# A list-scheduled attention and feed-forward kernel: other planner costs, 600 random trials of its priorities, and masks made by GpSimd and ScalarE

## The chip, the cores and the metric

One core of a Trainium2 chip runs the whole program. The metric is the device time of one execution in microseconds. The kernel before takes 627.38 us, the median of three runs (626.61 to 627.97).

## The reference

Sliding-window attention with sink keys is followed by a two-matrix feed-forward layer with an ELU between the matrices.

```python
batch, n_heads, seq, head_dim = (4, 8, 768, 64);  n_sink, window = (4, 128)
scores = scale * np.matmul(q, k.transpose(0, 1, 3, 2))
keep = is_sink | in_window                 # key < n_sink, or 0 <= query - key < window
a = softmax(np.where(keep, scores, -1e9))
x = np.matmul(a, v)                        # transposed and reshaped to 3072 tokens x 512
h = x @ w_in                               # 512 x 2048
g = np.where(h > 0.0, h, np.exp(np.minimum(h, 0.0)) - 1.0)
return g @ w_out                           # 2048 x 512
```

## The kernel before, in words

**Chunks.** The 24 query tiles of 128 tokens are cut into nine chunks of 2, 2, 2 and then 3 tiles (`SIZES`). For each chunk the attention of all heads makes `x`, and then the feed-forward layer runs over 16 slices of the hidden dimension: per slice, 12 matmuls into `h` (stage 1, L765) and, two slices later, the matmuls into `acc` (stage 2, L793). The first two chunks are taken in parts (`PARTS`): slices 0 to 6 of chunk 0, 0 to 12 of chunk 1, then the rest of both. A slice needs two pieces of weights.

**Attention of chunk 0.** Four pairs of heads with two query tiles each make eight units. A unit is: scores on PE (L601, `s`), a masked minimum on DVE (L616, `e`), exponentials on ACT (L618), a small addition on POOL or ACT (L622), a reciprocal on DVE (L623), a diagonal matrix on POOL (L630, `pq`), a product with it on PE that turns the probabilities round (L636, `acc`), a copy (L640, `pt`), and the product with the values on PE (L653, `po`). There are two score banks. There are two key buffers (`kqs`); those of pairs 2 and 3 are loaded into the buffers of pairs 0 and 1 once their scores are done (L516). Later chunks split the probabilities into two halves of float16 (L668, L669), turn them round by a DMA transpose (L687), and take the sinks' part on POOL (L675 to L679).

**Weights.** Each of the 32 pieces is loaded (L314, `raw`), split by ACT (L307, `wu`), DVE (L308, `wv`) and ACT (L456), and its low half is made by two subtractions on POOL (L457, `w`).

**Masks and parameters.** `n_sink` and `window` arrive by DMA, are cast by DVE (L1110), spread over the partitions by a small matmul (L1111) and copied back (L1112). `make_masks` makes the distances on POOL and DVE (L331 to L337) and the masks from them on DVE (L345, L348). PE takes the small matmul before the first scores.

**What sets the order.** Nothing above is issued in the order in which it is written. Every piece of work is a `Task` with an engine, a duration (`act_us`, `dve_us`, `pool_us` or a number), dependencies, and for PE a position. `Plan.order` gives each task a due time, counted back from the PE position of what needs it, and runs a list scheduler: an engine that is free takes, of what is ready, what is due first. This is repeated 8 times, each time with the PE times of the last round, and the round with the earliest end is kept. `HOP` is the planner's delay from one engine to the next. `keep_order` then pins the order of each engine to that plan, so that the engines wait for each other by semaphores but never swap instructions. Where the plan has PE idle in its first 100 us, `with_idle_products` puts products of a constant matrix on PE (L882, `hot`), as many as fill 60% of the gap at `IDLE_US` each.

**End.** A check of the ranges of all inputs runs beside the work. A second, general path is not taken here.

Of the kernel before, what the change touches and what calls it, by code (L numbers as in the profile page):

```python
# [12 lines left out]
I32 = mybir.dt.int32  # L13
# [7 lines left out]
P = 128  # L21
# [7 lines left out]
NS = 4  # L29
# [18 lines left out]
ROUNDS = 8  # L48
VISIT = 3
# [3 lines left out]
IDLE_US, IDLE_FILL, IDLE_UNTIL, IDLE_LEAST = 0.11, 0.6, 100.0, 0.8  # L53
# [3 lines left out]
PE_T, PE_V = 0.25, 0.25  # L57
# [46 lines left out]
class Plan:  # L104


    HOP = {"PE": 0.15, "ACT": 0.08, "DVE": 0.08, "POOL": 0.2, "SP": 0.0}
# [30 lines left out]
    def order(self):  # L138
# [7 lines left out]
        for _ in range(ROUNDS):  # L146
            self.backward()
            end = self.forward(pe)
            if VERBOSE:
                print("round", end)  # L150
            if best is None or end < best[0]:
                best = end, [(t.start, t, t.eng) for t in self.tasks]
        self.end = best[0]
        for s, t, e in best[1]:
            t.take(e)
            t.start = s
        return [t for _, t, _ in sorted(best[1], key=lambda v: (v[0], v[1].n))]
# [126 lines left out]
def act_us(n, scaled=False):  # L284
    return 0.17 + 0.00088 * n + (0.08 if scaled else 0.0)


def dve_us(n):
    return 0.12 + 0.00115 * n


def pool_us(n):
    return 0.18 + 0.0019 * n
# [32 lines left out]
def make_masks(nc, tmp, sk, low, m0, m1, m2):  # L326


    ri = tmp[:, 0:P].bitcast(I32)
    rel, own, prev = (tmp[:, i * P : (i + 1) * P] for i in (1, 2, 3))  # L330
    nc.gpsimd.iota(ri, pattern=[[-1, P]], base=0, channel_multiplier=1)  # L331
    for j in range(NS):
        nc.gpsimd.memset(sk[:, j : j + 1], float(j))
# [32 lines left out]
def fast_path(tc, ctx, first, kq, vx, wt, out, low, spread, numbers, flag):  # L366
# [36 lines left out]
    spread(po_ps[0])  # L403
# [4 lines left out]
    tmp = pts[-1].rearrange("p b k -> p (b k)").bitcast(F32)  # L408
    second, rest = make_masks(nc, tmp[:, : 4 * P], tmp[:, 4 * P : 4 * P + NS], low, m0, m1, m2)
    nc.gpsimd.memset(ones, 1.0)  # L410
    for t in wu:
        nc.gpsimd.memset(t, 0)
    nc.gpsimd.memset(hot, 1.0)
    make_identity(nc, ident)
# [11 lines left out]
    second_ = add("DVE", 0.65, second)  # L426
    rest_ = add("DVE", 0.5, rest)
    numbers_ = add("DVE", 1.3, numbers)
# [12 lines left out]
    def weights(k):  # L441
# [3 lines left out]
        ld = add("SP", 0.4, lambda: load_weights(nc, raw, wt[k]), deps=[w_done.get(k - AHEAD, [None])[0]], lat=1.45)  # L445
        if wide:
            steps = weight_f32(nc, v, top, raw, 2.0)
            a = add("ACT", act_us(512), steps[0], deps=[ld])
            b = add("DVE", 0.13 + 0.00108 * 512, steps[1], deps=[a], slow=1.5)
# [45 lines left out]
    def attention(c):  # L495
# [12 lines left out]
        def split_keys(h):  # L508
# [4 lines left out]
            if c < DUP:  # L513
                ld = None
                if (c, h) not in first["kq"]:
                    ld = add("SP", 0.4, lambda: nc.sync.dma_start(st[:, :kw], kq[:, o : o + kw]), lat=dma_us(P * kw * 4) * 1.15)  # L516
                users = []
                return st, None, ld, ld, users
# [653 lines left out]
```

## Time and profile before

| | |
|---|---|
| median of three runs | 627.38 us |
| the profiled execution, its own time | 628.19 us |
| its span, first to last instruction | 626.3 us |
| PE busy | 606.1 us (97%) |
| DVE, ACT, POOL busy | 462.3, 421.2, 294.7 us |

The share of busy time is a mean over stages that have different limits, so the rows below are by stage. The stages are cut at 4.98 us, where the first scores run on PE, and at 32.69 us, where the first matmul of the feed-forward layer runs.

### The profile page before, as it was taken

What the parts mean: (1) busy time and instruction counts of PE and PEld (TensorE: products, weight loads), DVE (VectorE), ACT (ScalarE), POOL (GpSimd) and SP (SyncE); (2) the same over time, 40 slices, a digit from 0 to 9 for tenths busy, and PEclk for the clock granted to TensorE, in tenths of its full rate; (3) what the DMA queues carried; (4) which work ended last, traced back from release to release, by engine and by line L of the source; (5) the groups of instructions that cost most, each with busy time, mean ns of one, the idle gap of its engine ahead of it and who ended that gap; (6) DMA issues with size and microseconds to landing.
All of it is one profiled execution on the core that took longest, in us unless ns stands there. A gap on an engine that the chain in (4) does not pass through costs nothing.

```text
span 626.3 us, 13397 instructions
## 1 busy us (share of the span) xinstructions
PE 606.1 (97%) x4504; PEld 359.4 (57%) x4504; DVE 462.3 (74%) x1206; ACT 421.2 (67%) x1192; POOL 294.7 (47%) x595
## 2 busy tenths in 40 slices
PE   6997999999999999999999999999999999999995
PEld 4664665667675555555555555555555555555552
DVE  7877677979878786688788988788877887543323
ACT  5887888879878876676667666676767666432221
POOL 4876689875445444344344445334324444222221
PEclk9898999999999999999999999999999999999998
DMA  8698977758656665586456865676655864413101
GB/s 293 210 248 199 298 243 192 209 139 223 145 127 157 162 146 103 94 216 181 125 153 177 230 139 159 130 197 136 166 125 124 209 144 107 115 50 92 55 2 53
DMA packets 122077, 98.24 MB, mean 157 GB/s; under 512 B 98324, under 2 KB 98324, under 8 KB 122004
## 3 DMA queue, kind: packets, MB, share of 16 engines
q1 hardware_dynamic: 122004, 97.34, 60.7%
q8 instruction: 37, 0.61, 0.4%
q14 instruction: 36, 0.29, 0.2%
HBM read 66.38 MB, written 7.34 MB: 118 GB/s over the span
## 4 chain that ended last, share of the span: by engine, by line
PE 91%; POOL 3%; DVE 2%; issue 2%; DMA 1%; ACT 1%; POOLq 0%; ACTq 0%
PE acc L793 39%; PE h L765 38%; PE po L701 5%; PE s L595 2%; PE s L596 2%; PE s L601 2%; POOL w L457 1%; PE h L882 1%; PE acc L636 1%; DMA pt<-pq 1%; DMA vs<-in_vx_dram 1%; PE po L706 1%; PE po L653 0%; DVE pt L334 0%; POOL pq L630 0%
## 5 line engine op out<-in xcount | busy, mean ns | idle before, releaser
L765 PE MATMUL h<-x,w 128*128 128x384 f16 (+1 forms) x1728 | 274.9, 309 | 2.4 <-DVE g L776 2.3
L765 PEld LDWEIGHTS <-w 128*128 128x128 f16 x1728 | 168.3, 98 | 94.8 <-issue 3.2
L786 POOL TENSOR_TENSOR gl<-g,gh 128x384 f16<-128x384 f32 (+1 forms) x144 | 128.7, 894 | 157.3 <-ACT gh L779 134.2
L793 PE MATMUL acc<-w,gh 128*128 128x512 f16 x768 | 192.7, 379 | 1.0 <-POOL w L457 1.0
L773 ACT ACTIVATE g<-h 128x384 f32<-128x384 f32 (+1 forms) x144 | 65.1, 452 | 101.8 <-PE h L765 92.2
L793 PEld LDWEIGHTS <-gh 128*128 128x128 f16 x768 | 72.9, 98 | 69.4 <-issue 0.9
L793 PE MATMUL acc<-w,gl 128*128 128x512 f16 x384 | 109.2, 379 | 0.0
L669 DVE SCALAR_TENSOR_TENSOR pq<-e,st,pq 128x256 f16<-128x256 f32 (+1 forms) x176 | 95.1, 571 | 13.0 <-ACT pq L668 12.7
L618 ACT ACTIVATE e<-e,st 128x264 f32<-128x264 f32 (+1 forms) x192 | 92.9, 484 | 12.2 <-DVE st L616 11.2
L779 ACT ACTIVATE gh<-g 128x384 f16<-128x384 f32 (+1 forms) x144 | 69.3, 481 | 43.2 <-DVE g L776 41.5
L616 DVE CUSTOM_DVE_ANT_0 e<-s,m 128x264 f32<-128x264 f32 (+1 forms) x192 | 71.7, 405 | 26.2 <-PE s L596 19.8
L776 DVE SCALAR_TENSOR_TENSOR g<-g,h 128x384 f32<-128x384 f32 (+1 forms) x144 | 72.8, 506 | 13.2 <-POOL g L775 11.3
L668 ACT ACTIVATE pq<-e,st 128x256 f16<-128x256 f32 (+1 forms) x176 | 77.1, 482 | 5.3 <-DVE st L623 4.1
L775 POOL TENSOR_SCALAR g<-g 128x384 f32<-128x384 f32 (+1 forms) x80 | 41.5, 518 | 80.2 <-ACT g L773 79.8
L775 DVE TENSOR_SCALAR g<-g 128x384 f32<-128x384 f32 (+1 forms) x64 | 26.8, 419 | 65.7 <-ACT g L773 65.4
L793 PEld LDWEIGHTS <-gl 128*128 128x128 f16 x384 | 37.5, 98 | 46.6 <-POOL gl L786 0.9
L524 ACT ACTIVATE kq<-kqs 128x780 f16<-128x780 f32 (+1 forms) x48 | 42.7, 901 | 15.7 <-PE s L596 12.2
L457 POOL TENSOR_TENSOR w<-wv,w 128x256 f16<-128x256 f32 x64 | 49.2, 789 | 5.4 <-ACT w L456 4.7
L622 POOL TENSOR_SCALAR st<-st 128x2 f32<-128x2 f32 x84 | 21.2, 253 | 48.0 <-ACT e L618 44.1
L701 PE MATMUL po<-pt,vh 128*64 128x128 f16 x656 | 35.8, 221 | 2.6 <-DVE x L740 1.9
L618 ACT ACTIVATION_READ_ACCUMULATOR e<-e,st 128x1 f32 x192 | 36.1, 188 | 0.0
L595 PE MATMUL s<-kq 128*128 128x264 f16 (+1 forms) x144 | 34.3, 267 | 0.6 <-ACT x L739 0.6
(92 smaller groups left out, 628.8 us busy)
## 6 DMA issues: line engine op xcount, KB each, us to landing
raw<-in_wt_dram SPq DMA_DIRECT2D x32, 512.0 KB, 4.8
kqs<-in_kq_dram SPq DMA_DIRECT2D x24, 456.0 KB, 3.6
kqs<-in_kq_dram SPq DMA_DIRECT2D x24, 390.0 KB, 3.6
vs<-in_vx_dram SPq DMA_DIRECT2D x28, 256.0 KB, 3.6
out_dram<-wv SPq DMA_DIRECT2D x24, 256.0 KB, 2.6
vm<-in_kq_dram SPq DMA_DIRECT2D x24, 228.0 KB, 3.7
vm<-in_kq_dram SPq DMA_DIRECT2D x24, 195.0 KB, 3.4
vm<-in_vx_dram SPq DMA_DIRECT2D x6, 768.0 KB, 5.3
```

The costliest lines, as they stand in the source:

```text
L616: red = add("DVE", 0.24 + 0.001 * wd, lambda ee=ee, me=me, sp=sps[e], m=m, wd=wd, to_score=to_score: nc.vector.tensor_tensor_reduce(ee, sp ...
L618: ex = add("ACT", 0.47 + 0.00085 * wd, lambda ee=ee, me=me, rs=rs[:, e : e + 1]: nc.scalar.activation(ee, ee, AF.Exp, bias=me, scale=-1.0, ...
L668: a = add("ACT", act_us(nb * P, True), lambda src=src, hi=hi, re=re: nc.scalar.activation(hi, src, AF.Copy, scale=re), deps=[rr])
L669: b = add("DVE", 0.478 if nb == 2 else 0.33, lambda src=src, hi=hi, lo=lo, re=re: nc.vector.scalar_tensor_tensor(lo, src, re, hi, ALU.mult ...
L701: nc.tensor.matmul(po[e * D : (e + 1) * D, oc], vts[i][x][:, vo : vo + D], pt[:, (2 * e + part) * nb + i, :], start=new, stop=last)
L765: nc.tensor.matmul(hp[:, :n], win[:, part, d, :], xx[:, :n], start=k == 0, stop=k == 3 * ND - 1)
L773: a = add("ACT", act_us(n) + 0.18, lambda gf=gf, hp=hp, sums=sums: nc.scalar.activation(gf, hp[:, :n], AF.Exp, scale=1.0 / G_SCALE, accum_ ...
L775: b = add("DVE", 0.14 + 0.00057 * n, lambda gf=gf: nc.vector.tensor_scalar(gf, gf, -1.0, G_SCALE, ALU.add, ALU.mult), deps=[a], slow=2.1, ...
L776: b = add("DVE", dve_us(n), lambda gf=gf, hp=hp: nc.vector.scalar_tensor_tensor(gf, gf, 0.0, hp[:, :n], ALU.min, ALU.max), deps=[b])
L779: th = add("ACT", act_us(n), lambda gf=gf, gh=gh: nc.scalar.activation(gh[:, :n], gf, AF.Copy), deps=[b])
L786: tls.append(add("POOL", pool_us(cut), lambda gl=gl, gf=gf, gh=gh, cut=cut: nc.gpsimd.tensor_tensor(gl[:, :cut], gf[:, :cut], gh[:, :cut], ...
L793: nc.tensor.matmul(acc[i], gg[:, i * P : (i + 1) * P], wout[:, part, :], start=f == f0 and k == 0, stop=f == f1 - 1 and k == 2)
```

## The change

It alters five things; the line numbers below are of the kernel before.

1. All durations in the plan, and the delays `HOP`. Most become smaller; the DMA transposes become longer.
2. After the eight rounds come 600 further ones (`SEARCH`). Each takes the best plan so far, shifts by random amounts the due times of the tasks in some stretch of it (or all), or the PE positions of one kind of work, schedules again, and keeps the result if its planned end is no later.
3. The masks: GpSimd makes both distances itself, in float32. DVE keeps the comparisons. ScalarE casts the two parameters. In the plan the masks for units 1 and 2 follow the minimum of units 0 and 1, and the check of the parameters (`numbers`) follows the first exponentials of the feed-forward layer.
4. The first keys are the first DMA; the parameters follow them.
5. The constant products before 12 us of the plan are planned at twice the time, so fewer fit. For chunks 3 to 8 the small addition of L622 is always on POOL. The small matmul of the parameters stands first on PE by a pinned order.

```diff
-PE_T, PE_V = 0.25, 0.25
+PE_T, PE_V = 0.25, 0.13
...
-    HOP = {"PE": 0.15, "ACT": 0.08, "DVE": 0.08, "POOL": 0.2, "SP": 0.0}
+    HOP = {"PE": 0.2, "ACT": 0.14, "DVE": 0.125, "POOL": 0.09, "SP": 0.0}
...
+        draw = random.Random(1)
+        for _ in range(SEARCH):
+            _, due, ideal, then = best
+            for t, d, s in zip(self.tasks, due, then):
+                t.due, t.start = d, s[0]
+            for t, i in zip(pe, ideal):
+                t.ideal = i
+            a, w, by = draw.uniform(0.0, 200.0), draw.choice((5.0, 15.0, 40.0)), draw.choice((0.5, 2.0, 6.0))
+            kind = draw.random()
+            if kind < 0.65:
...
+                for t, s in zip(self.tasks, then):
+                    if a <= s[0] < a + w:
+                        t.due += draw.gauss(0.0, by)
+            else:
...
+            best = self.better(best, pe)
...
 def act_us(n, scaled=False):
-    return 0.17 + 0.00088 * n + (0.08 if scaled else 0.0)
+    return 0.085 + 0.000855 * n + (0.095 if scaled else 0.0)
...
 def dve_us(n):
-    return 0.12 + 0.00115 * n
+    return 0.067 + 0.00105 * n
...
-    ri = tmp[:, 0:P].bitcast(I32)
-    rel, own, prev = (tmp[:, i * P : (i + 1) * P] for i in (1, 2, 3))
-    nc.gpsimd.iota(ri, pattern=[[-1, P]], base=0, channel_multiplier=1)
...
-    nc.vector.tensor_copy(rel, ri)
-    nc.vector.tensor_scalar(own, rel, 0.0, 1.0e6, ALU.is_lt, ALU.mult)
-    nc.vector.tensor_tensor(own, own, rel, ALU.add)
-    nc.vector.tensor_scalar(prev, rel, float(P), None, ALU.add)
+    own, prev = tmp[:, 0:P], tmp[:, P : 2 * P]
+    nc.gpsimd.iota(own, pattern=[[-1, P]], base=0, channel_multiplier=1, **exact)
+    nc.gpsimd.affine_select(out=own, in_=own, compare_op=ALU.is_ge, fill=1.0e6, base=0, pattern=[[-1, P]], channel_multiplier=1)
...
+    nc.gpsimd.iota(prev, pattern=[[-1, P]], base=P, channel_multiplier=1, **exact)
...
+                if c < DUP:
+                    rr = add("ACT", 0.18, eps[0], deps=[ex for _, ex in exps], or_=("POOL", 0.21, eps[1]))
+                else:
+                    rr = add("POOL", 0.21, eps[1], deps=[ex for _, ex in exps])
...
+            us = IDLE_US if t.start > COLD_UNTIL else 2 * IDLE_US
...
-            nc.vector.tensor_copy(t[0:1, :], ints[0:1, :])
+            nc.scalar.activation(t[0:1, :], ints[0:1, :], AF.Copy)
...
+            if n == "kqs" and i == 0:
+                nc.sync.dma_start(ints[0:1, 0:2], n_sink.bitcast(I32))
+                nc.sync.dma_start(ints[0:1, 2:4], window.bitcast(I32))
```

**VectorE at the start of the program.** `pt` holds the distances here, `words` the parameters, `m` the masks; the ISA rows are the minimum of unit 0. Before:

```order
L334 CAST pt_112<-pt_112 128x128
L335 TENSOR_SCALAR pt_112<-pt_112 128x128
L337 TENSOR_SCALAR pt_112<-pt_112 128x128
L336 TENSOR_TENSOR pt_112<-pt_112 128x128
L1110 CAST words<-words 1x4
L1112 COPY words<-po_172 128x4
L345 TENSOR_SCALAR m_183<-pt_112,words 128x4
L345 TENSOR_SCALAR m_181<-pt_112,words 128x128
L345 TENSOR_SCALAR m_182<-pt_112,words 128x128 x2
...
L616 ISA e_95,st_98<-s_170,m_181 128x132
```

After:

```order
L1146 COPY words<-po_172 128x4
L371 TENSOR_SCALAR m_180<-pt_112,words 128x4
L371 TENSOR_SCALAR m_178<-pt_112,words 128x128
L374 TENSOR_TENSOR m_178<-m_178,m_180 128x4
L642 ISA e_95,st_98<-s_170,m_178 128x132
```

Five instructions ahead of the parameters' copy are gone from this engine, and of the masks only that of unit 0 is ahead of its minimum.

**TensorE at the scores of head pairs 2 and 3 of chunk 0.** `s` are scores, `acc<-pq,e` the turning product, `po<-pt,vs` the product with the values. Before, from the first scores of pair 2 to those of pair 3:

```order
L601 MATMUL s_170<-kqs_63 128x132
L601 MATMUL s_171<-kqs_63 128x132
L636 MATMUL acc_174<-pq_104,e_95 128x128 x4
L601 MATMUL s_170<-kqs_63 128x264
L601 MATMUL s_171<-kqs_63 128x264
L653 MATMUL po_172<-pt_109,vs_65 64x128 x2
L653 MATMUL po_172<-pt_110,vs_65 64x128 x2
L653 MATMUL po_172<-pt_110,vs_66 64x128 x2
L601 MATMUL s_170<-kqs_64 128x132
L601 MATMUL s_171<-kqs_64 128x132
```

After, from the last turning product of pair 1 on:

```order
L668 MATMUL acc_174<-pq_104,e_95 128x128 x4
L685 MATMUL po_172<-pt_109,vs_63 64x128 x2
L685 MATMUL po_172<-pt_110,vs_63 64x128 x2
L685 MATMUL po_172<-pt_110,vs_64 64x128 x2
L627 MATMUL s_170<-kqs_61 128x132
L627 MATMUL s_171<-kqs_61 128x132
...
L627 MATMUL s_170<-kqs_61 128x264
L627 MATMUL s_171<-kqs_61 128x264
...
L627 MATMUL s_170<-kqs_62 128x132
L627 MATMUL s_171<-kqs_62 128x132
```

All work of pairs 0 and 1 now stands ahead of pair 2; where lines are left out stand 6 and 7 constant products.

**GpSimd in the attention of chunk 0.** `pq<-ident,st` are the diagonals, `w<-wv,w` the low halves of weights. Before, from the third diagonal to the sixth:

```order
L630 TENSOR_TENSOR pq_106<-ident,st_100 128x256
L622 TENSOR_SCALAR st_101<-st_101 128x2
L457 TENSOR_TENSOR w_138<-wv_126,w_138 128x256
L630 TENSOR_TENSOR pq_104<-ident,st_101 128x256
L457 TENSOR_TENSOR w_138<-wv_126,w_138 128x256
L457 TENSOR_TENSOR w_137<-wv_125,w_137 128x256
L457 TENSOR_TENSOR w_140<-wv_124,w_140 128x256 x2
L622 TENSOR_SCALAR st_102<-st_102 128x2
L457 TENSOR_TENSOR w_137<-wv_125,w_137 128x256
L630 TENSOR_TENSOR pq_105<-ident,st_102 128x256
```

After, the same stretch:

```order
L662 TENSOR_TENSOR pq_106<-ident,st_100 128x256
L650 TENSOR_SCALAR st_101<-st_101 128x2
L662 TENSOR_TENSOR pq_104<-ident,st_101 128x256
L483 TENSOR_TENSOR w_136<-wv_124,w_136 128x256 x2
L483 TENSOR_TENSOR w_138<-wv_126,w_138 128x256 x2
L483 TENSOR_TENSOR w_137<-wv_125,w_137 128x256 x2
L650 TENSOR_SCALAR st_102<-st_102 128x2
L483 TENSOR_TENSOR w_140<-wv_124,w_140 128x256 x2
L662 TENSOR_TENSOR pq_105<-ident,st_102 128x256
```

The four diagonals of pairs 0 and 1 now come ahead of all weights, and six halves of weights in a row stand behind the fourth. Counted over the whole queue, 20 halves stand ahead of the first subtraction of the feed-forward layer (L786 before) where 14 stood, 26 ahead of the seventh where 28 stood, and 64 (all) ahead of the 23rd where 52 stood. The constant products number 22 (3, 6, 7 and 6 in a row) where there were 29 (7, 9, 5, 4 and 4); all of them stand ahead of the first feed-forward matmul.

## Rows read from the trace of the kernel before

**Rows 1.** Stretches of the span: length, busy us (instructions) by engine, granted clock, DMA share, GB/s.

```profile
0.00:4.98 4.98, 0.48 (x2) 0.49 (x2) 3.08 (x5) 1.28 (x1) 3.03 (x23) 1.00 0.52 153
4.98:14.10 9.12, 8.90 (x49) 5.70 (x49) 7.09 (x40) 5.76 (x19) 2.84 (x7) 1.00 0.94 358
14.10:24.20 10.10, 8.78 (x65) 6.13 (x63) 7.70 (x24) 8.49 (x24) 9.07 (x14) 0.83 0.69 219
24.20:32.69 8.49, 7.98 (x66) 5.28 (x65) 7.30 (x26) 7.19 (x22) 6.00 (x13) 1.00 0.67 199
32.69:66.00 33.31, 27.77 (x256) 17.61 (x256) 25.52 (x76) 27.46 (x81) 24.36 (x52) 0.95 0.96 245
66.00:115.00 49.00, 47.96 (x362) 30.57 (x361) 36.26 (x85) 41.60 (x116) 39.99 (x71) 1.00 0.78 236
115.00:620.00 505.00, 504.25 (x3715) 293.62 (x3712) 374.78 (x954) 329.44 (x934) 209.44 (x417) 1.00 0.57 138
620.00:626.30 6.30, 0.00 (x0) 0.00 (x0) 0.55 (x1) 0.00 (x0) 0.00 (x0) 0.68 0.38 133
```

**Rows 2.** Waits of TensorE: engine, line, releaser, us in total, times, longest us.

```profile
PE po L1111 <- DVE words L1110: 4.5, 1, 4.5
PE h L765 <- DVE g L776: 2.3, 3, 1.2
...
PE acc L793 <- POOL w L457: 1.0, 2, 0.6
```

**Rows 3.** Timeline, first 7 us, VectorE and GpSimd: start us, us, what, [idle before].

```profile
3.32 0.28 POOL masks.py:199 TENSOR_SCALAR_AFFINE_SELECT ident<-ident 128x128 f32<-128x128 f32 x1
...
1.23 2.46 DVE L334 CAST pt<-pt 128x128 f32<-128x128 int32 x1 [1.23 <-POOL pt L331]
3.72 0.23 DVE L335 TENSOR_SCALAR pt<-pt 128x128 f32<-128x128 f32 x1
...
4.20 0.15 DVE L1110 CAST words<-words 1x4 f32<-1x4 int32 x1
...
6.62 0.29 DVE L616 CUSTOM_DVE_ANT_0 e<-s,m 128x132 f32<-128x132 f32 x1
```

**Rows 4.** Timeline, SyncE's queue of DMA issues, first 3 us.

```profile
0.73 0.34 SPq L1125 DMA_DIRECT2D words<-in_n_sink_dram  x1
...
1.40 0.36 SPq L1136 DMA_DIRECT2D kqs<-in_kq_dram  x1
```

**Rows 5.** Line L516 between 8 and 13 us, keys of pairs 2 and 3.

```profile
L516 SPq DMA_DIRECT2D kqs<-in_kq_dram x2: 327/328/328, 8.6 to 12.6; - x2
...
DMA to landing us min/median/max: 2.7/4.3/5.9
```

**Rows 6.** Timeline of TensorE, 5 to 33 us.

```profile
7.24 1.25 PE L601 MATMUL s<-kqs 64*128 64x264 f32 x4
...
16.53 0.50 PE L601 MATMUL s<-kqs 64*128 64x132 f32 x4
...
23.54 0.71 PE L601 MATMUL s<-kqs 64*128 64x264 f32 x4
...
32.69 2.79 PE L765 MATMUL h<-x,w 128*128 128x256 f16 x24
```

**Rows 7.** Timeline of VectorE at the minimum of unit 7.

```profile
24.28 0.43 DVE L616 CUSTOM_DVE_ANT_0 e<-s,m 128x264 f32<-128x264 f32 x1 [0.21 <-PE s L601]
...
24.99 0.16 DVE L623 RECIPROCAL st<-st 128x2 f32<-128x2 f32 x1
```

**Rows 8.** Groups by line, first 115 us: count | busy us, mean ns | idle before.

```profile
L457 POOL TENSOR_TENSOR w<-wv,w 128x256 f16<-128x256 f32 x52 | 39.5, 780 | 5.3 <-ACT w L456 4.7
...
L307 ACT ACTIVATE wu<-raw 128x512 f16<-128x512 bf16 x27 | 20.4, 772 | 2.9 <-DMA raw<-in_wt_dram 2.9
...
L456 ACT ACTIVATE w<-wv 128x512 f16<-128x512 f32 x26 | 16.2, 623 | 2.1 <-DVE wv L308 1.7
```

**Rows 9.** Line L622 on ScalarE, its small addition.

```profile
L622 ACT ACTIVATE st<-st x12: 203/203/204, 274.0 to 530.3; 128x2 f32<-128x2 f32 x12
```

More of the change, by code (lines that the diff above doesn't have):

```diff
@@ L147, in order, with better @@
             self.backward()
[L148 to L152, printed above, removed]
+            best = self.better(best, pe)
[9 more added lines that the diff above has]
+            if kind < 0.65:
+                if kind < 0.25:
+                    self.backward()
+                    a, w, by = 0.0, 1.0e9, draw.choice((0.3, 1.0, 3.0))
+                for t, s in zip(self.tasks, then):
+                    if a <= s[0] < a + w:
+                        t.due += draw.gauss(0.0, by)
+            else:
+                line, by = draw.choice((0, 1, 2, 3)), draw.gauss(0.0, by)
+                for t in pe:
+                    if t.line == line and a <= t.ideal < a + w and draw.random() < 0.7:
+                        t.ideal += by
+            best = self.better(best, pe)
         self.end = best[0]
-        for s, t, e in best[1]:
+        for t, (s, e) in zip(self.tasks, best[3]):
             t.take(e)
             t.start = s
-        return [t for _, t, _ in sorted(best[1], key=lambda v: (v[0], v[1].n))]
+        return sorted(self.tasks, key=lambda t: (t.start, t.n))
+    def better(self, best, pe):
+        due, ideal = [t.due for t in self.tasks], [t.ideal for t in pe]
+        end = self.forward(pe)
+        if VERBOSE:
+            print("round", end)
+        if best is None or end <= best[0]:
+            best = end, due, ideal, [(t.start, t.eng) for t in self.tasks]
+        return best
     def report(self):
@@ L424, in slot @@
         return turn[name] % RINGS[name]
-    second_ = add("DVE", 0.65, second)
-    rest_ = add("DVE", 0.5, rest)
-    numbers_ = add("DVE", 1.3, numbers)
+    second_ = add("DVE", 0.55, second)
+    rest_ = add("DVE", 0.4, rest)
+    numbers_ = add("DVE", 1.1, numbers)
     nc1, nc2 = len(SIZES) * NF, (2 * len(SIZES) - DUP) * NP
@@ L679, in sinks @@
                         nc.gpsimd.tensor_tensor(hi[:, 1, :], flat, hi[:, 0, :], ALU.subtract)
[L681 removed]
+                    b = add("POOL", 0.6, sinks, deps=[rr], lock=False)
                     parts.append(b)
@@ L888 @@
 VERBOSE = False
-HINTS = dict(PE=8, ACT=110, DVE=120, SP=50)
+HINTS = dict(PE=8, ACT=122, DVE=120, SP=50)
 E = mybir.EngineType
@@ L906, in with_idle_products @@
         if t.start - free > IDLE_LEAST and ready < free + IDLE_LEAST:
-            extra[i] = [Task("PE", IDLE_US, product, (nxt.bank,), [], 0.0, None, 1.0) for _ in range(int(IDLE_FILL * (t.start - begin) / IDLE_US))]
+            us = IDLE_US if t.start > COLD_UNTIL else 2 * IDLE_US
+            extra[i] = [Task("PE", us, product, (nxt.bank,), [], 0.0, None, 1.0) for _ in range(int(IDLE_FILL * (t.start - begin) / us))]
         free = t.start + t.dur
@@ L923, in keep_order @@
     seen = len(bb.instructions)
-    prev = {}
+    prev = {ins.engine: ins.name for ins in bb.instructions if ins.engine == E.PE}
     base = tc.cur_priority
```

66 lines of the change are left out of this document (34 added, 32 removed).

## The prediction

> **What bounds the kernel now.** I read the stretches first. From 115 to 620 us TensorE works 504.25 of 505.00 us at a granted clock of 1.00, which is its upper level of 2.4 GHz [rows 1]. There the sum of the matmuls is the time, no matmul is added or taken away, and no order can gain more than the 0.75 us of idle time. The 6.3 us after 620, output and end, hold no matmul and no edited step. What an order can change is therefore ahead of 115 us, in four parts: the 4.98 us before the first scores; 27.71 us of chunk 0's attention, from 4.98 to 32.69, in which TensorE looks busy (8.90 of 9.12, 8.78 of 10.10, 7.98 of 8.49 us) but partly with constant products and at half rate; 33.31 us in which feed-forward slices run while later attention and the weights are still being made, with 33.31 - 27.77 = 5.5 us idle and a granted clock of 0.95; and 49 us with 49.00 - 47.96 = 1.0 us idle [rows 1].
>
> The waits say who is late [rows 2]. The longest is the first: 4.5 us for DVE's cast of the parameters. Next come 2.3 us in three waits for an ELU step on DVE, and two waits, 1.0 us, for a weight's low half from POOL. In the 33.31 us DVE, ACT and POOL are busy 25.52, 27.46 and 24.36 us [rows 1]: none is full, ACT is nearest at 82%. TensorE waits there for chains through three queues, that is, for the order.
>
> **The start.** DVE's first instruction, a cast of 128x128 integers, takes 2.46 us from 1.23 to 3.69, where the next one of that size takes 0.23; the cast of the parameters behind it runs at 4.20 [rows 3]. After the change DVE does neither. ScalarE's cast of four numbers is not in the trace; the bounds are 0.15 us (the same cast on DVE) and 0.20 us (ScalarE's small addition) [rows 3, 9], and I take 0.2. GpSimd gets two or three more instructions ahead of its first diagonal, of which the trace has the like of one, an affine select at 0.28 us [rows 3]; I take 0.3 each, between 0.1 and 0.6, so GpSimd's preparation ends some 0.5 us later than the 3.60 where it ends now (0.3 to 1.8 later). The keys are issued at 0.73, where `n_sink` stood, instead of 1.40, and the parameters behind them [rows 4]. I put the first scores at 4.3 instead of 4.98 (3.9 to 5.2). Of the six mask steps ahead of unit 0's minimum (6.62) four go behind it, at about 0.23 us each: 0.7 + 0.9 = 1.6 us earlier, so 5.0.
>
> Why the long cast matters: it ends 0.09 us after GpSimd's last preparation (3.32 + 0.28 = 3.60), though it began while GpSimd was already at work [rows 3]. So what GpSimd does can hold a DVE copy. The Trainium skill says so too (SBUF — State Buffer, Who interferes with whom): the pair of ports that the two share is an exclusive lock, and the later of the two blocks fully; tensor_scalar, which the mask comparisons are, is among the operations it lists. By that rule the comparisons would wait for GpSimd's longer preparation and begin only when it ends. By the rows that end is 4.1 (3.9 to 5.4) and the comparisons come at 4.6, so I count nothing and keep 0.8 us as the upper end.
>
> **Chunk 0's attention.** Little of those 1.6 us survives as such, because pair 2 meets a fixed date. Its keys are issued at 8.6 us and land 5.9 us later, at 14.4; those of pair 3, issued at 12.6, land after 2.7, at 15.3 [rows 5]. DMA is 94% busy from 4.98 to 14.10 [rows 1], the five weight loads stand ahead of these keys in SP's queue before and after, so an earlier issue lands hardly earlier: I take 14.4 (13.5 to 14.6). Before, pair 2's first scores run at 16.53, behind work of pair 1 [rows 6]. After, all work of pairs 0 and 1 stands ahead of them, and with four diagonals in a row on GpSimd and the lead of 1.6 us I expect that work to be through at about 14. So pair 2 starts at 14.5: 2.0 us earlier.
>
> From there to unit 7's scores it took 23.54 - 16.53 = 7.0 us, with a turning product and three value products between the scores [rows 6]. After, only constant products stand between, and the score banks set the pace: scores at 23.54, banks read at 24.99, so 1.45 us a turn for the larger unit [rows 6, 7], about 1.1 for the smaller by two minima that are each 0.43 - 0.29 = 0.14 us shorter. Three turns are 1.1 + 1.45 + 1.1 = 3.65 us; two weight steps of DVE and an `x` stand between the minima in its new order, up to 1.9 us. So unit 7 comes at 14.5 + 3.65 + 1.6 = 19.8, 3.7 us earlier (5.5 at best). The rest, 32.69 - 23.54 = 9.15 us to the first feed-forward matmul, keeps its parts. Against it stand six halves in a row on GpSimd behind the fourth diagonal, 6 x 0.78 = 4.7 us [rows 8]. They begin at about 13 and end at 17.7, when unit 4's exponentials are just done, and two more halves then hold its diagonal to some 20. That is still before unit 7's scores, so I charge 0.3 us. **First term: 3.4 us earlier**, a first feed-forward matmul at 29.3. Bounds: 5.5 (nothing in the way), and 1.0 (every half from the block shows).
>
> **The first feed-forward slices.** By the order, 20 halves of weights are done on GpSimd ahead of the first subtraction instead of 14, and 26 instead of 28 ahead of the seventh. So 6 halves instead of 14 fall into slices 1 to 7: 8 x 0.78 = 6.2 us less for GpSimd, and for ACT 4 pieces x (0.77 + 0.62) = 5.6 us less out of 27.46 [rows 1, 8]. This work is not gone: three of the four pieces must now be made by ACT in the shortened attention before, where ACT was already busy 8.49 of 10.10 and 7.19 of 8.49 us. What the stretch can give is 5.5 us of idle time and, at half of TensorE's rate for a tenth of 33.31 us, 1.7 us more. I take under a third of these 7.2: **second term, 2.0 us**, between a gain of 6 and a loss of 2 (if ACT comes late with the three pieces).
>
> **The weights later on.** All 64 halves are done ahead of the 23rd subtraction where 52 were. The two waits of 1.0 us [rows 2] should go, if nothing new comes: **third term, 0.5 us** (0 to 1.0). New durations for chunks 2 to 8 and the fixed place of the small addition move work that lies beside TensorE (DVE 374.78, ACT 329.44, POOL 209.44 of 505.00 us): nothing, with the cover being two slices of lead; if the cover is gone, see the fourth rival.
>
> **The sum.** 3.4 + 2.0 + 0.5 = 5.9 us, so the span goes from 626.3 to 620.4. The profiled execution took 628.19 us, 1.89 more than its span, and the median of the runs is 0.81 below it: 628.19 - 5.9 - 0.81 = 621.5 us. Its own range, with the first term at 1.9 to 4.5 and the second at 0.5 to 4, is 618 to 624.5.
>
> **The rivals.**
> - *Given back.* ACT was 82% busy in the 33.31 us and is 41.60 of 49.00 us busy in the next 49 [rows 1]. If it cannot do better, three pieces earlier only shift its lateness: the first term stays at 2, the others at 0, and the time is 625.4. For it: three engines are loaded at once. Against it: DVE and ACT together wait ahead of 32.69 for single chains, as the start shows.
> - *More.* The 5.5 and 1.7 us of the third stretch go nearly whole, with 5 us in the first term and 1.0 in the third: 12 us, 615.4. Against it: ACT would then have to be over 95% busy for 60 us.
> - *Half rate.* Scores of the larger unit took 1.25 us at 7.24 and 0.71 at 23.54 [rows 6], so TensorE was at its lower level, 1.2 GHz, in the first, though the row of that stretch says 1.00 [rows 1]; it had been idle for 4.5 us just before [rows 2]. The stretch from 14.10 has a granted clock of 0.83, so a part of it was at 1.2 GHz too, and TensorE had been idle for 1.3 us of it [rows 1]. Before, 16 constant products stood in the first 10 us; now 3 do, and TensorE has a gap before 14.4. If the lower level holds through most of chunk 0's attention and returns in the first slices, a pair's two score groups cost about 0.9 us more, and its turning and value products about 2, by the same ratio; over pairs 1 to 3 that is 8.5 us, about half of it on the path, 4.3 us, and 1 us in the slices. That is more than the first term, and with the second at 0 the time is 628.8, slower than before. It decides once the stretch at 1.2 GHz is longer than about 14 us. For it: the lost products. Against it: after the gap comes a dense stretch of products.
> - *A tight plan.* The new durations have less reserve. If each of the 96 slices of chunks 3 to 8 (16 x 6) waited 0.08 us, that is 7.7 us, and the time is 629.2. Against it: 0.75 us of idle time in 505 now.
>
> The Trainium skill holds (TensorE: Matmul & The Clock Gate, What's actually happening) that a gate on the array's clock follows how busy the array has recently been, and passes half of the pulses otherwise. This agrees with the 1.25 and 0.71 us; by the rule alone, fewer products in the cold start mean the third rival's 628.8.
>
> **How the numbers follow.** Chances: forecast 0.58, given back 0.20, more 0.09, half rate 0.07, tight plan 0.06. A measurement of this kernel tells about 0.2%, 1.25 us, from no change. Faster than 626.1: the forecast, more, and four fifths of given back, 0.83. Same: 0.05, from given back and the tight plan. Slower than 628.6: 0.12, from half rate and most of the tight plan. The range leaves out part of "more" below, and the two slow cases above: 616.0 to 626.6.
>
> **What would show it.** In the new profile: the first scores at 4.3 and unit 0's minimum at 5.0; pair 2's scores at 14.5; unit 7's at 19.8; the first feed-forward matmul at 29.3; under 4 us of idle TensorE between there and the end of the stretch; no wait for `w`; the stretch up to 620 us as full as now. Wrong would be: pair 2's scores after 15.5, a granted clock under 0.8 over the attention, or more than 2 us of idle TensorE after 115 us.

## The result and the profile after

The change makes the kernel slower: 631.74 us (median of five, 631.08 to 633.69) against 627.57 us (626.61 to 628.07), a ratio of 1.0077 [1.006, 1.0093]. The prediction was 621.5, faster. The profiled execution took 631.08 us with a span of 629.3, so 3.0 us more span than before.

The stretches of the changed kernel, cut where those of [rows 1] are cut: at the first scores (5.72), the first feed-forward matmul (34.36) and the same dates behind it. Each line gives the length, the busy us (and instructions) of TensorE, of its weight loads, of VectorE (DVE), ScalarE (ACT) and GpSimd (POOL), the granted clock, the DMA share and GB/s.

```profile
0.00:5.72 5.72, 0.49 (x3) 0.50 (x3) 0.00 (x0) 1.49 (x2) 3.45 (x22) 1.00 0.61 184
5.72:14.10 8.38, 7.45 (x31) 4.50 (x31) 5.76 (x30) 5.12 (x19) 2.12 (x4) 1.00 0.94 349
14.10:24.20 10.10, 8.06 (x66) 5.79 (x64) 7.48 (x23) 9.40 (x25) 8.85 (x13) 1.00 0.56 199
24.20:34.36 10.16, 8.82 (x71) 6.03 (x71) 9.40 (x26) 9.73 (x31) 10.00 (x15) 1.00 0.92 333
34.36:66.00 31.64, 28.13 (x272) 17.88 (x270) 28.98 (x94) 30.68 (x96) 25.55 (x58) 1.00 1.03 241
66.00:115.00 49.00, 45.65 (x336) 28.41 (x334) 38.32 (x77) 43.41 (x115) 45.69 (x70) 0.97 0.82 248
115.00:620.00 505.00, 504.74 (x3720) 294.02 (x3718) 370.20 (x949) 320.26 (x911) 208.32 (x415) 1.00 0.56 135
620.00:629.30 9.30, 2.80 (x14) 0.94 (x12) 2.34 (x7) 0.85 (x2) 0.67 (x1) 0.79 0.26 90
```

After 115 us TensorE is as full as it was. The first feed-forward matmul is 1.67 us later. In the stretch behind it TensorE idles 31.64 - 28.13 = 3.51 us where it idled 5.54, at a granted clock of 1.00 instead of 0.95. From 66 to 115 it idles 3.35 us where it idled 1.04, with the clock at 0.97, and GpSimd, 39.99 us busy before, is busy 45.69 of 49.00. So time is lost ahead of 34 us, won up to 66 and lost again up to 115. Counted in matmuls, 3720 + 14 are left after 115 us where 3715 were: 19 more at 0.136 us (504.25 / 3715) are 2.6 of the 3.0 us.

TensorE's waits in the changed kernel (releaser, us in total, times, longest):

```profile
PE po L1145 <- ACT words L1144: 5.2, 1, 5.2
PE s L627 <- DVE st L642: 3.6, 7, 0.7
PE h L797 <- POOL w L483: 2.3, 1, 2.3
```

The longest is still the parameters' chain, now through ScalarE instead of DVE [rows 2]. ScalarE's first instruction in the kernel before, and its first two in the changed one, from the timelines:

```profile
0.74 1.28 ACT L618 ACT_TABLE_LOAD   x1 [0.74 <-PEq L1163]
```

```profile
3.59 1.28 ACT L1144 ACT_TABLE_LOAD   x1 [3.59 <-DMA words<-in_window_dram]
4.88 0.20 ACT L1144 ACTIVATE words<-words 1x4 f32<-1x4 int32 x1
```

The load of ScalarE's function table stands ahead of the cast, and it waited for the parameters' DMA as the cast did; before, it ran at the start of the program, at 0.74 us, long before anything needed it. The Trainium skill (ScalarE: Activation LUTs, What ACT_TABLE_LOAD costs) has 1283 ns for the load, as the row has, and 1380 ns of drain with it at every switch to a different set. Here the cast begins 0.01 us behind the program's first load, so no drain shows between the two.

TensorE in chunk 0's attention, its timeline:

```profile
5.72 0.81 PE L627 MATMUL s<-kqs 64*128 64x132 f32 x4
...
10.37 1.22 PE L668 MATMUL acc<-pq,e 128*128 128x128 f32 x4
11.52 1.25 PE L627 MATMUL s<-kqs 64*128 64x264 f32 x4
12.70 0.69 PE L685 MATMUL po<-pt,vs 128*64 128x128 f32 x4
13.33 2.17 PE L668 MATMUL acc<-pq,e 128*128 128x128 f32 x12
...
16.24 1.16 PE L668 MATMUL acc<-pq,e 128*128 128x128 f32 x8
17.90 0.44 PE L685 MATMUL po<-pt,vs 128*64 128x128 f32 x4 [0.51 <-DVE x L772]
18.50 0.66 PE L685 MATMUL po<-pt,vs 128*64 128x128 f32 x8 [0.16 <-DVE pt L672]
19.09 0.49 PE L627 MATMUL s<-kqs 64*128 64x132 f32 x4
...
24.11 0.71 PE L627 MATMUL s<-kqs 64*128 64x264 f32 x4 [0.61 <-DVE st L642]
...
34.36 1.47 PE L797 MATMUL h<-x,w 128*128 128x256 f16 x12
```

Pair 2's first scores are at 19.09 (16.53 before, [rows 6]), right behind the last value product of pair 1. That product ran, in the kernel before, behind pair 2's first scores, with these ahead of it:

```profile
17.84 1.85 PE L636 MATMUL acc<-pq,e 128*128 128x128 f32 x8 [0.82 <-POOL pq L630]
19.63 1.25 PE L601 MATMUL s<-kqs 64*128 64x264 f32 x4
20.81 1.21 PE L653 MATMUL po<-pt,vs 128*64 128x128 f32 x12
```

Pair 2's keys had landed long before 19.09 (line L542 of the changed kernel, to be held against [rows 5]): issued at 8.7, landed 5.6 us later, at 14.3.

```profile
L542 SPq DMA_DIRECT2D kqs<-in_kq_dram x2: 328/328/328, 8.7 to 12.8; - x2
...
DMA to landing us min/median/max: 2.8/4.2/5.6
```

And GpSimd and TensorE about 105 us, two timelines:

```profile
100.58 1.79 POOL L483 TENSOR_TENSOR w<-wv,w 128x256 f16<-128x256 f32 x2
102.33 0.85 POOL L818 TENSOR_TENSOR gl<-g,gh 128x256 f16<-128x256 f32 x1
103.14 0.38 POOL L707 TENSOR_TENSOR st<-e,st 128x8 f32<-128x8 f32 x1
...
104.42 4.12 POOL L483 TENSOR_TENSOR w<-wv,w 128x256 f16<-128x256 f32 x5
```

```profile
105.19 0.72 PE L797 MATMUL h<-x,w 128*128 128x256 f16 x5 [2.31 <-POOL w L483]
...
107.53 2.65 PE L797 MATMUL h<-x,w 128*128 128x256 f16 x12
```

The low halves of weights (w) that GpSimd makes from 66 to 115 us, in the kernel before (L457) and in the changed one (L483), by stretch: length, busy us (instructions), clock, DMA share, GB/s:

```profile
66.00:115.00 49.00, 20.80 (x27) 1.00 0.78 236
```

```profile
66.00:115.00 49.00, 25.71 (x33) 0.97 0.82 248
```

Six halves more, 4.9 us of GpSimd's time, stand in a stretch in which it had 9 us to spare. About 105 us it works without a pause, and TensorE waits 2.31 us for the first of five halves. Twelve matmuls that take 1.47 us at 34.36 then take 2.65: behind the wait TensorE falls to its lower level of 1.2 GHz (granted clock 0.66 from 105 to 110 us).

Three groups of the first 115 us show what the plan had too short (count | busy us, mean ns | idle before):

```profile
L483 POOL TENSOR_TENSOR w<-wv,w 128x256 f16<-128x256 f32 x61 | 47.6, 800 | 2.2 <-ACT w L482 1.9
...
L337 DVE SCALAR_TENSOR_TENSOR wv<-raw,wu 128x512 uint32<-128x512 uint32 x31 | 28.2, 923 | 3.6 <-ACT wu L336 2.8 <-POOL w L483 0.5 <-issue 0.2
...
L701 DVE SCALAR_TENSOR_TENSOR pq<-e,st,pq 128x256 f16<-128x256 f32 x27 | 16.2, 626 | 1.9 <-ACT pq L700 1.9
```

The plan of the changed kernel has 0.155 + 0.00186 x 256 = 0.631 us for the first, 0.61 for the second and 0.396 for the third. Added up over all tasks, the plan of the changed kernel has 399 us of work for VectorE, 388 for ScalarE and 250 for GpSimd; the profile of the same kernel has 462.5, 420.9 and 304.6 us busy. In the plan of before they were 485, 502 and 268 against 462.3, 421.2 and 294.7: too long on two engines, too short on the third.

These sums hold the tasks' own durations alone, and the comparison is not quite like with like. While it schedules, the planner makes a GpSimd task and a VectorE task with `slow` above 1 wait for each other (`lock` in `forward`), and the three groups above are of this kind. Worked out from the kernels' own plans, these waits add 38 us for VectorE and 18 for GpSimd in the changed kernel (31 and 21 before). If the profile's durations hold such waits too, as the 2.46 us cast of [rows 3] suggests, the changed plan is short by some 5, 8 and 12%, and not by 14, 8 and 18%.

### The profile page after: what moved, and what is told of

It is laid out like the page before. It is cut to its first block, busy times and chain, and to the rows that moved or that the text cites. A ratio compares the mean times of both kernels' runs of the same rounds, so it can differ in the third digit from the quotient of the medians.

```text
span 629.3 us, 13374 instructions
## 1 busy us (share of the span) xinstructions
PE 606.1 (96%) x4497; PEld 358.1 (57%) x4497; DVE 462.5 (73%) x1202; ACT 420.9 (67%) x1193; POOL 304.6 (48%) x593
## 4 chain that ended last, share of the span: by engine, by line
PE 80%; DVE 5%; ACT 5%; POOL 5%; issue 3%; DMA 0%; SPq 0%; DVEq 0%; ACTq 0%; POOLq 0%
PE acc L825 35%; PE h L797 35%; PE po L733 4%; POOL w L483 2%; PE s L621 2%; PE s L622 2%; ACT e L646 1%; DVE pq L701 1%; POOL gl L818 1%; DVE e L642 1%; DVE wv L337 1%; ACT wu L336 1%; ACT w L482 1%; ACT pq L700 1%; PE s L627 1%
## 5 line engine op out<-in xcount | busy, mean ns | idle before, releaser
L818 POOL TENSOR_TENSOR gl<-g,gh 128x384 f16<-128x384 f32 (+1 forms) x144 | 127.0, 882 | 181.8 <-ACT gh L811 156.8
L701 DVE SCALAR_TENSOR_TENSOR pq<-e,st,pq 128x256 f16<-128x256 f32 (+1 forms) x176 | 100.6, 599 | 17.3 <-ACT pq L700 16.6
L808 DVE SCALAR_TENSOR_TENSOR g<-g,h 128x384 f32<-128x384 f32 (+1 forms) x144 | 72.7, 505 | 16.3 <-POOL g L807 14.5
L807 DVE TENSOR_SCALAR g<-g 128x384 f32<-128x384 f32 (+1 forms) x67 | 24.9, 371 | 62.7 <-ACT g L805 62.2
L807 POOL TENSOR_SCALAR g<-g 128x384 f32<-128x384 f32 (+1 forms) x77 | 43.3, 563 | 36.8 <-ACT g L805 36.1
L483 POOL TENSOR_TENSOR w<-wv,w 128x256 f16<-128x256 f32 x64 | 49.8, 796 | 2.3 <-ACT w L482 1.9
L551 DVE SCALAR_TENSOR_TENSOR kq<-kqs,kq 128x396 f16<-128x396 f32 (+1 forms) x48 | 32.3, 677 | 5.4 <-ACT kq L550 5.0
```

The source lines that it names most:

```text
L483: tls = [add("POOL", pool_us(256), lambda c=c: nc.gpsimd.tensor_tensor(w[k][:, 1, c], v[:, c], w[k][:, 0, c], ALU.subtract), deps=[th]) fo ...
L701: b = add("DVE", 0.396 if nb == 2 else 0.265, lambda src=src, hi=hi, lo=lo, re=re: nc.vector.scalar_tensor_tensor(lo, src, re, hi, ALU.mul ...
L807: b = add("DVE", 0.06 + 0.00057 * n, lambda gf=gf: nc.vector.tensor_scalar(gf, gf, -1.0, G_SCALE, ALU.add, ALU.mult), deps=[a], slow=2.1, ...
L808: b = add("DVE", dve_us(n), lambda gf=gf, hp=hp: nc.vector.scalar_tensor_tensor(gf, gf, 0.0, hp[:, :n], ALU.min, ALU.max), deps=[b])
L818: tls.append(add("POOL", pool_us(cut), lambda gl=gl, gf=gf, gh=gh, cut=cut: nc.gpsimd.tensor_tensor(gl[:, :cut], gf[:, :cut], gh[:, :cut], ...
```

## Experiments

The theories at the outset: A, the new durations are too short, so that the plan counts on engines that come late; B, the search fits the order to the plan's errors; C, the new start loses. Times are medians, ratios against runs of the kernel before on the same chip.

**e1: the cast on VectorE.**

```diff
-            nc.scalar.activation(t[0:1, :], ints[0:1, :], AF.Copy)
+            nc.vector.tensor_copy(t[0:1, :], ints[0:1, :])
```

> The changed kernel with the cast of the parameters back on VectorE; order of everything else the same. Theory A (the new durations are too short for engines that share a port, so the chosen order has no reserve): the first scores come about 1.3 us earlier, at 4.4, because ScalarE's table load no longer waits for the parameters; the keys of pair 2 still land at about 14.4 and the later waits stay, so the time is 630 to 631.7 (changed kernel: 631.7). Theory B (the 600 rounds fit the plan to its own errors): the same. Theory C (the new start is the loss): 627 to 628.5.

Measured: 630.95 us, 1.0065 [1.0044, 1.0086]. The wait for the parameters falls from 5.2 to 4.2 us, and the median by 0.8, which the two intervals do not tell from nothing. By that the table load at the start is about a fifth of the loss; the 2.3 us wait for `w` stays, so C is not the whole.

**e2: the changed kernel without the search.**

```diff
-        draw = random.Random(1)
-        for _ in range(SEARCH):
...
-            best = self.better(best, pe)
```

> The changed kernel with no random rounds (SEARCH = 0). Theory A: no better, 630 to 634, with a wait for a weight's low half or for VectorE of over 2 us somewhere before 115 us. Theory B: 625 to 628. Theory C: as A.

Measured: 632.31 us, 1.0077 [1.006, 1.0094]. The loss is all there without one random round, so B falls. It took another form than A expected: behind the wait for the parameters no single wait is over 2 us, but five are for an ELU step (3.8 us in all, 1.0 at most), beside others. The stretches of this kernel:

```profile
33.00:66.00 33.00, 30.07 (x275) 18.36 (x273) 29.62 (x95) 32.04 (x97) 26.66 (x55) 1.00 1.01 227
66.00:115.00 49.00, 45.23 (x355) 28.77 (x351) 40.93 (x81) 42.36 (x111) 47.78 (x71) 1.00 0.81 252
```

GpSimd is busy 47.78 of 49.00 us, 29.97 of it with 36 halves, and TensorE idles 3.8 us there.

**e3 and e4: old durations in the changed kernel; new durations alone in the kernel before.**

```diff
-    HOP = {"PE": 0.2, "ACT": 0.14, "DVE": 0.125, "POOL": 0.09, "SP": 0.0}
+    HOP = {"PE": 0.15, "ACT": 0.08, "DVE": 0.08, "POOL": 0.2, "SP": 0.0}
...
-    return 0.067 + 0.00105 * n
+    return 0.12 + 0.00115 * n
...
```

(e3, against the changed kernel; e4 is the kernel before with all these lines the other way round.)

> The changed kernel with all planned durations and delays of the kernel before; masks, first keys and 600 rounds as changed. Theory A: 625.5 to 628, most of the loss gone, and what is left of it the 0.7 us of the start. Theory B: 630 to 632. Theory C: 630 to 632.

> The kernel before with only the new durations and delays; old masks, old start, no random rounds. Theory A: 629 to 633, slower than before by most of the 4.2 us. Theory B and theory C: 626 to 628, no change.

Measured: e3 627.6 us, 0.9999 [0.9983, 1.0015]; e4 629.17, 1.0019 [0.9999, 1.0039]. With the old durations the loss is gone, as A said. But the durations alone bring only 1.4 of the 4.2 us, and that is hardly told from nothing. A was not the whole.

**e5 and e6: the masks, the start and the fewer constant products alone; the search alone,** both in the kernel before with its old durations. e5 also has the small addition of chunks 3 to 8 fixed on GpSimd.

> The kernel before with the masks, the first keys, the fewer constant products and their hints alone; old durations, eight rounds, no random search. Theory A (the new durations are what loses): the old durations keep the loss away, so the time is that of the kernel before or up to 1.5 us less, 626 to 628. Theory C (the new start itself loses some 3 us, since the parameters wait for ScalarE's table): 629 to 631.

> The kernel before with the 600 random rounds alone. Theory A: with the old durations the search neither loses nor gains much, 625.5 to 628. Theory B (the search fits the order to the errors of the plan): at least 1.5 us slower than before, 629 to 632.

Measured: e5 631.98 us, 1.0065 [1.0042, 1.0088]; e6 629.2, 1.002 [1.0003, 1.0036]. Both were misses for A. The edits of e5 lose 4 us by themselves, somewhat more than C gave them. The search loses 1 on its own, at the edge of what B gave it (629 to 632); on top of e5 it gives e3, 4.4 us less; on top of e2 it gives the changed kernel, 0.6 less. So it moves the time by some us either way, and the edits of e5 do too: with the search on, they gain 1.6 us (e6 to e3), though these two intervals overlap.

**e7 and e8: planned sums equal to the measured busy times; another start of the random numbers.** e7's edit, before the plan is made:

```diff
+BUSY = {"DVE": 1.16, "ACT": 1.085, "POOL": 1.2}
...
+        for t in self.tasks:
+            t.dur *= BUSY.get(t.eng, 1.0)
+            t.ways = {e: (d * BUSY.get(e, 1.0), f) for e, (d, f) in t.ways.items()}
```

> The changed kernel with every planned duration of VectorE multiplied by 1.16, of ScalarE by 1.085 and of GpSimd by 1.2, so that the planned sums equal the busy times of the profile (463, 424 and 296 us against 462, 421 and 295 to 305). Theory A: most of the 4.2 us come back, 626 to 628.5, and no wait of TensorE for a weight's low half is over 1 us. Rival D (the time of an order is a lottery of some 3 us, whatever the durations): anywhere from 626 to 633, with no relation to the sums.

> The changed kernel with another start of the random numbers, so another order out of the same durations. Theory A: slow again, 630 to 633, since the durations are as short as before. Rival D (a lottery): it can as well come out at 627 or 628; a difference of over 2 us from the changed kernel would show that single orders scatter by about as much as the whole effect.

Measured: e7 625.64 us, 0.9973 [0.9959, 0.9987]; e8 631.34, 1.0054 [1.0035, 1.0073]. Three factors turn the slower kernel into a faster one, and another random start does not.

**e9 to e12: e7 without the search (e9), with the other random start (e10), with e1's edit (e11); and factors 1.25, 1.17 and 1.3 (e12).**

> e7 (planned sums made equal to the measured busy times) without the 600 random rounds. Theory E (both are needed: the search helps only where the planned durations are as long as the measured ones): 2 to 4 us slower than e7's 625.6, so 628 to 630. Rival F (right sums are enough): within 1 us of e7, 625 to 626.6.

> e7 with the other start of the random numbers. Theory E: 625 to 627, as the same durations lead the search to an order that holds on the chip. Rival D (single orders are a lottery of some 3 us, e7 drew a good one): 628 to 631.

> e7 with the parameters cast by VectorE, so that ScalarE loads its table while it has nothing else to do. First scores 1.2 to 1.3 us earlier, at about 4.5. If the start were on the path: 624.3; since pair 2's keys land at a date of their own, I expect a third of it, 624.8 to 625.4.

> The changed kernel with the durations multiplied by 1.25 (VectorE), 1.17 (ScalarE) and 1.3 (GpSimd), so that the planned sums lie 7 to 9 per cent above the measured busy times. Theory E: reserve does no harm as long as the plan still fits the time, 625 to 627.5. Rival F2 (only sums equal to the measured ones are good): 628 to 631.

Measured: e9 624.16 us, 0.9939 [0.992, 0.9957]; e10 624.73, 0.995 [0.9932, 0.9969]; e11 624.63, 0.9949 [0.9931, 0.9967]; e12 630.94, 1.0047 [1.0033, 1.0061]. E falls: the factors are enough, and the search adds nothing to them. So does D, the lottery: the three orders from the short durations (the changed kernel, e2, e8) lie at 631.3 to 632.3 us, the three from the multiplied ones (e7, e9, e10) at 624.2 to 625.6. A as "too short" is not the whole, since e12, with sums 7 to 9% longer than the profile's, is nearly as slow as the changed kernel; that is one order, with the search, and was not run without it. Of three sizes the middle one is best. That it is the right one holds for the durations alone: with the planner's own waits for the lock (48 us for VectorE, 30 for GpSimd) e7's plan has 511, 424 and 326 us against 456.3, 422.1 and 302.3 busy. In e12 the loss sits elsewhere; first e9's stretches, then e12's:

```profile
33.00:66.00 33.00, 29.94 (x288) 19.78 (x285) 29.22 (x94) 30.86 (x97) 24.20 (x52) 1.00 1.03 253
66.00:115.00 49.00, 48.09 (x379) 31.25 (x378) 38.37 (x83) 44.91 (x131) 42.38 (x66) 1.00 0.91 262
```

```profile
33.00:66.00 33.00, 27.27 (x237) 17.43 (x238) 26.10 (x82) 27.31 (x87) 24.21 (x51) 0.95 1.05 235
66.00:115.00 49.00, 49.00 (x397) 31.66 (x395) 37.51 (x84) 45.09 (x126) 40.17 (x67) 1.00 0.83 254
```

Against e2, e9 has 288 + 379 matmuls done in these 82 us where e2 has 275 + 355, and GpSimd 42.38 us busy in the second stretch instead of 47.78. e12 leaves TensorE idle 5.7 us in the first stretch and none in the second, as if too little were ready early. Why its plan orders the work so is open.

The first feed-forward matmul, in e9 and then in e5:

```profile
34.18 2.79 PE L772 MATMUL h<-x,w 128*128 128x256 f16 x24
```

```profile
31.46 2.03 PE L768 MATMUL h<-x,w 128*128 128x256 f16 x12
```

In the kernel before it came at 32.69 [rows 6]. So e9 begins the layer 1.5 us later and is 3.7 us faster, and e5 begins it 1.2 us earlier and is 4 us slower: how early the layer begins does not settle the time, what follows up to 115 us counts for more.

**e13 to e15: which engine's durations, and the masks under multiplied durations.** e13 is e9 without the mask, start and product edits and without the fixed small addition; e14 and e15 are e2 with the factors of e7 for GpSimd alone, and for VectorE and ScalarE alone.

> The kernel before with the new durations multiplied as in e7, without the mask edits and without the search. If the mask edits and the new start lose by themselves (e5 was 4 us slower than before): 622 to 623.5, less than e9's 624.2. If e5's loss came from its old durations (an accident of the order): within 1.2 us of e9, 623.5 to 625.5. If the mask edits gain what the prediction gave them at the start: 626 to 628.

> The changed kernel without the search (632.3) with GpSimd's durations alone multiplied by 1.2. Theory G (GpSimd's durations carry it, since TensorE's longest wait in the changed kernel is for a low half of a weight): 624 to 627. Theory H (VectorE and ScalarE carry it, as their planned sums were 63 and 33 us short and GpSimd's 45 to 55): 630 to 633. Both in part: 627 to 630.

> The changed kernel without the search with VectorE's and ScalarE's durations alone multiplied, by 1.16 and 1.085. Theory G: 630 to 633. Theory H: 624 to 627. Both in part: 627 to 630.

Measured: e13 621.3 us, 0.9903 [0.9884, 0.9922], the fastest of all; e14 627.86, 0.9999 [0.9986, 1.0011]; e15 626.04, 0.9963 [0.9948, 0.9979]. From e2's 632.3, GpSimd's durations give back 4.4 us, the other two engines' 6.3, and all three together 8.1 (e9). The mask and start edits lose 624.16 - 621.3 = 2.9 us here too. e13's stretches:

```profile
33.00:66.00 33.00, 30.29 (x280) 19.39 (x280) 28.40 (x76) 31.62 (x96) 27.70 (x52) 1.00 1.03 273
66.00:115.00 49.00, 49.00 (x388) 31.97 (x386) 41.43 (x86) 44.48 (x127) 44.50 (x67) 1.00 0.83 243
115.00:620.00 505.00, 497.48 (x3654) 288.66 (x3653) 365.85 (x942) 321.92 (x927) 204.72 (x386) 1.00 0.56 134
```

No idle time from 66 to 115, and 3654 matmuls left for the time after, against 3715 [rows 1]: 61 x (504.25 / 3715 =) 0.136 us = 8.3 us; the span is 7.3 us shorter.

**e16 to e18: the table load and the constant products under multiplied durations.** e16 is e9 with e1's edit; e17 is e16, and e18 is e13, with one line:

```diff
-            us = IDLE_US if t.start > COLD_UNTIL else 2 * IDLE_US
+            us = IDLE_US
```

(e17; e18 has the opposite edit.)

> e9 (right sums, no search, 624.2) with the parameters cast by VectorE, so that the table load is out of the way; the version that should be fastest. The first scores come 0.6 to 1.2 us earlier. From e11 against e7 (1.0 us less): 623.2 to 624.2.

> e16 (623.3) with the constant products before 12 us planned at their old time, so 10 of them instead of 5 ahead of the fourth scores; nothing else moves. Theory K (the missing products keep TensorE at 1.2 GHz): the upper level comes 2 to 5 us earlier than e16's 15.4 us and the time is 0.5 to 2 us less, 621.3 to 622.8. Rival L (the rest of the edits loses, the order of the attention): 622.9 to 623.7, whatever the clock does.

> e13 (621.3, 22 constant products in its first 11 us) with the constant products before 12 us planned at twice the time, as the change does, so 10 of them; nothing else moves. Theory K: the upper level of the clock comes later than e13's 8.5 us, at 11 to 16, and the time is 0.5 to 2.5 us more, 621.8 to 623.8. Rival L: 620.8 to 621.8.

Measured: e16 623.26 us, 0.992 [0.9903, 0.9937]; e17 622.6, 0.9909 [0.9886, 0.9931]; e18 621.97, 0.9909 [0.9889, 0.9928]. e16 is 0.9 us below e9, much as e1 was below the changed kernel (0.8) and e11 below e7 (1.0): no pair is clear of noise, but all three agree. The products move the time by 0.7 us each way, in the direction of theory K, but the intervals of e13 and e18, and of e16 and e17, overlap: unclear. The traces of e13 and e18 do differ. TensorE in e13, with 22 constant products (`hot`), then in e18, with 10:

```profile
8.18 1.55 PE L890 MATMUL h<-hot 128*128 128x240 bf16 x12
9.66 0.50 PE L605 MATMUL s<-kqs 64*128 64x132 f32 x4
...
11.41 1.90 PE L644 MATMUL acc<-pq,e 128*128 128x128 f32 x12
...
30.31 2.79 PE L773 MATMUL h<-x,w 128*128 128x256 f16 x24
```

```profile
8.16 1.38 PE L890 MATMUL h<-hot 128*128 128x240 bf16 x6
9.48 0.81 PE L605 MATMUL s<-kqs 64*128 64x132 f32 x4
...
12.07 2.93 PE L644 MATMUL acc<-pq,e 128*128 128x128 f32 x12
...
31.96 2.25 PE L773 MATMUL h<-x,w 128*128 128x256 f16 x19
```

The same twelve turning products take 1.90 and 2.93 us: with the products TensorE is at 2.4 GHz by 9.66 us, without them still at 1.2 GHz at 12, and the feed-forward layer begins 1.65 us later. In e17 ten products did not do as much: there the twelve took 2.93 us too, as in e16, so its 0.7 us are not K's.

**What is shown, and what is open.** The multiplied durations, whose sums without the planner's waits match the measured ones, are worth about 8 us against the change's own (e4 to e13 7.9, e2 to e9 8.1, with the search 6.1), 6.5 against the old ones (before to e13). That it is the match of the sums that does it is argued: only three sizes were run, and the longest only once. The mask, start and product edits lose 2.9 us or more without the search (e13 to e9 2.9, e4 to e2 3.1, before to e5 4). Of that the table load is about 0.9, the products perhaps 0.7. What loses the remaining 1 to 2 us is open: the order in chunk 0's attention that the scheduler makes of the new start (in e13 pair 2's scores stand at 14.83, ahead of pair 1's last products), or the small addition now fixed on GpSimd. These were not run apart, and with the old durations and the search the same edits gained 1.6. The parts do not add up: durations alone lose 1.4 us, masks alone 4, both 4.5, and with the search on top 4.2. The version to keep is e13: the new durations multiplied, nothing else of the change.

## Why the prediction was wrong

**The start: failed by 1.4 us.** GpSimd's preparation ends as foretold (4.02 us by its timeline, against 4.1), and ScalarE's cast takes the 0.20 that I had. But the first scores came at 5.72, not 4.3, since the table load was nowhere in the sum; with the cast on VectorE (e1) it runs at 0.74 us and the first scores at 4.68. In the trace of before it ran at 0.74 us, ahead of a wait that came much later, and cost nothing. I costed the moved instruction and not what must precede it on its new engine.

**Chunk 0's attention: failed by 3.2 us.** The date of the keys was right (14.4 foretold, 14.3). What failed is "I expect that work to be through at about 14", said of pairs 0 and 1. From the first scores to pair 2's I had 14.5 - 4.3 = 10.2 us; it took 19.09 - 5.72 = 13.37. In the trace of before the last value product of pair 1 ran at 20.81, so I had asked for 7 us where the order won about 2. TensorE was at its lower level for much of this work: four turning products took 1.22 us at 10.37, eight took 1.16 at 16.24. By the rows at the upper level (1.16 for eight turning products, 0.71 for the scores at 24.11, 0.44 for the value products at 17.90) the four rows from 10.37 to 13.33 take some 1.8 us more than they would there, an estimate. The waits for an `x` and a `pt` add 0.7. From pair 2's scores on, the reckoning held: 5.0 us to unit 7's (I had 5.3), 10.25 to the feed-forward layer (9.5). The first term was 1.7 us of loss instead of 3.4 of gain.

**The first feed-forward slices: right in sign, too small.** Idle time fell by 2.0 us and the half rate went with it (0.05 x 33.31 = 1.7 us): 3.7, where I took 2.0 and had an upper bound of 6.

**The weights later on: wrong in sign, by 4.3 us.** The first term missed by more, 5.1 us, and with either of the two right the sum would have come out faster. But the experiments point here: e9 begins the feed-forward layer at 34.18, nearly as late as the changed kernel, loses 0.9 us of idle time from 66 to 115 where that loses 3.35, and is faster than before. I expected the waits for `w` to go and the new durations to cost "nothing, with the cover being two slices of lead", since I looked for that cover after 115 us. From 66 to 115 the stretch lost 2.3 us of idle time and 0.03 x 49 = 1.5 us at half rate, 3.8 instead of a gain of 0.5. That all 64 halves come ahead of the 23rd subtraction, where I saw the waits go, seems to be what crowds GpSimd there: 33 halves instead of 27, beside the subtractions and the sinks of the later chunks, each longer than the plan has it (in the first 115 us 0.82 and 1.03 us, in the plan 0.631 and 0.6). The count alone is not it: e13 makes 31 there (25.63 us) and has no idle time.

The three terms give 1.7 - 3.7 + 3.8 = 1.8 of the 3.0 us by which the span grew; the rest is not found in them.

**The rivals.** The tight plan named the cause, durations without reserve, and its price (629.2) was the nearest; but it put the place after 115 us, where 0.26 us are idle, and had a chance of 0.06. It was also only half the truth: the masks lose without it (e5), and more reserve lost as well (e12). Half rate came as that rival said, with fewer products and a longer stretch at 1.2 GHz at the start (e18 against e13), but did not turn the sign. The lapse before (granted clock 0.83 from 14.10, [rows 1]) did not come back, and it had cost 1.2 us in two rows alone: eight turning products took 1.85 us at 17.84 and the scores 1.25 at 19.63, where 1.16 and 0.71 are the upper level's. "Given back" happened in its way, by GpSimd and not by ScalarE, and 6 us further than I had it.

**What I should have seen.** The trace of before had the check on every new number of the diff: 780 ns for a half of a weight [rows 8] against 0.631 in the new plan, which adds only its own waits for the lock to that. I used the trace for the cost of what moved, and never held the planner's own durations against it.

## What to carry to other kernels

Before a planner's durations are changed, add them up by engine and hold the sums against the busy times of the profile, with and without the waits that the planner adds by itself. Here durations whose sums were 8 to 18% too short cost 6 to 8 us of 630, in one run some 7 to 9% too long cost 5, and a search through 600 orders could not make up for it. A search is as good as the plan that it minimises, so it should be judged by the chip. And for an instruction that is moved to another engine, what must come first there belongs in the sum.

## What the runs showed of the hardware

- ScalarE's table load waited for the parameters' DMA where the first activation behind it did: 1.28 us at 3.59 in the changed kernel, at 0.74 before and in e1, whose first activation is an exponential. Whether an early activation that needs nothing would hide it was not tried.
- The same twelve matmuls took 1.90 us with 22 constant products ahead of them and 2.93 with 10, and the first feed-forward matmul moved by 1.65 us. The two profiled executions differ by 1.4 us (620.78 and 622.16), the medians by 0.7.
